# Four consecutive tokens to a partition in the router of a fused retention and mixture-of-experts kernel

## The chip, the cores and the metric

The kernel runs on one core of one Trainium2 chip. The metric is the device time of one execution in microseconds (us), the median of several runs.

The engines are named as the profile names them: PE is TensorE (matmul), PEld its weight loads, DVE is VectorE, ACT is ScalarE, POOL is GpSimd, SP is SyncE, which here only issues DMA transfers. A line number such as L471 points into the kernel that was profiled; the same statement has another number in another version.

## The reference, cut to what matters

```python
# attention: q, k, v are (8 batches, 8 heads, 576 tokens, 64)
scores = matmul(q, k.T) / sqrt(64)
ret = scores * Dmat[head]            # causal, decays as gamma[head] ** distance
x = matmul(ret, v)                   # -> (4608 tokens, 512)

# mixture of experts: 8 experts, 512 -> 1024 -> 512
logits = x @ w_gate
noisy  = logits + log1p(exp(x @ w_noise)) * noise     # noise: (4608, 8)
top2   = the two largest of noisy, with softmax weights
out[t] = sum over its two experts e of  weight * (relu(x[t] @ w1[e]) @ w2[e])
```

## The kernel before: the parts that matter

Attention is done in 16 **units** (a batch and half of its heads), four for each pair of batches. After a pair is done, its 1152 tokens are **routed**: gate logits, noise, top two, the place of each token in its expert's list. A route is a generator, and its pieces are put between the pieces of the next four units. A route holds its tokens as 9 columns of 128. After the third and the fourth route five **early** tiles of experts run between the pieces of the fourth route, then the 35 remaining tiles, the **expert stage**.

One unit's step in program order, cut:

```python
for n in range(NU + 1):
    if u + 4 < NU:
        at.load(u + 4, (nc.sync,) * 3)         # raw_q, raw_k, raw_v: 1.57 MB a unit
    if n in (1, 2):
        rt.load_noise(n - 1)                   # two batches of 9 transfers
    at.scores(u, 0)                            # PE; DVE masks the scores out of PSUM
    step()                                     # a piece of the pending route
    at.out(p)                                  # previous unit: x = S v, ACT copies it to xT
    at.tr(u + 1, "q")                          # PE transposes, ACT copies QT
    at.scores(u, 1)
    at.cast(u + 2)                             # POOL: kn, qb; ACT: vn from raw_v
    at.tr(u + 1, "k")                          # ACT copies KT
    at.states(u)
    ...
```

In the traces each engine takes its instructions in the program's order. A late raw_v thus holds ACT in `cast`, and the KT behind it, which the next unit's scores need (PE waits 2.97 us for KT at 49.1 us).

The four parts that the change touches (cuts marked with "..."):

```python
# (1) noise: 16 transfers of 32 partitions x 8 batches x 32 bytes, and two for the tails
nq = nm[:, :512, :].rearrange("b (c q r) e -> q r b c e", q=32, r=4)
for r in (2 * j, 2 * j + 1):
    for c in range(4):
        nc.sync.dma_start(out=self.noise[r * 32:r * 32 + 32, :, c, :], in_=nq[:, r, :, c, :])
nc.sync.dma_start(out=self.noiset[j * HD:(j + 1) * HD], in_=nt[:, j])

# (2) a route's rows of x: PE transposes back, ACT takes them out of PSUM (9 a route)
nc.scalar.activation(xr[c // 3][:, c % 3, :DM // 2].bitcast(BF16), pt, Act.Copy)

# (3) one-hots, twice a route; PE multiplies oh by olo to invert the permutation
V.tensor_tensor(olo[:, j], self.iota..., lo[:, j]..., Alu.is_equal)
for c in range(C):                             # C = 9
    V.tensor_scalar(oh[:, j, c, :], self.iota[:, :NH], hi[:, j, c:c + 1], K["local"][:, c:c + 1],
                    Alu.is_equal, Alu.mult)

# (4) ahead of the expert stage: gathers of its first tiles into attention's raw_q buffers
for i in range(3):
    xg = raw.tile([P, 2, 4, P], F32, name="raw_q")...
    nc.gpsimd.memset(xg, 0.0)
    for s in range(2):
        gather(tc, keep, xd, xg, i, s)
    pre.append(xg)
```

The raw_q buffers are four; the five early tiles use them too. The expert stage has a buffer "xg" of its own for the tiles that are not pre-gathered.

## Time and profile before

| | before |
|---|---|
| time, median of the first 3 runs | 514.96 us (514.65 to 515.98) |
| span of the profiled run | 515.2 us |
| mean granted PE clock | 0.900 |
| 0 to 49 us, start and units 0 to 3 | 49.1 us |
| 49 to 177 us, units 4 to 15 with three routes | 127.7 us |
| 177 to 231 us, fourth route and early experts | 54.1 us |
| 231 to 242 us, the first tile of the expert stage | 11.1 us |
| 242 to 515 us, the rest of the expert stage | 273.1 us |

The prediction below shows the lines on which its argument rests. Here are four others: from the page of the kernel before the totals, two of its slice rows (each digit is the busy share, or the granted clock, of one fortieth of the span in tenths), and the group of the rows of x (line, engine, operation, out<-in, shapes, count; then busy us, ns of one; then idle time ahead of it).

```profile
PE 420.6 (82%) x4587; PEld 304.6 (59%) x4627; DVE 248.4 (48%) x685; ACT 282.6 (55%) x429; POOL 278.9 (54%) x389
...
PE   0576777687589487895999999999999999999960
...
PEclk9999578666767699898999999999999999999995
...
L492 ACT ACTIVATE xr<-tr 128x512 bf16<-128x512 bf16 x36 | 21.3, 594 | 3.8 <-issue 2.9
```

The total of 82% hides two stages. PE is full from the 20th slice on, and hardly anywhere to the left of it; there its clock (the share of full speed that the throttle granted) is only 0.5 to 0.7 in many slices. Only the left half can give time to a change outside the expert stage.

### The profile page before, as it was taken

The numbers are of one execution on the slowest core, as the hardware profiler recorded it, in microseconds if no ns is written. First come the engines' busy times: TensorE is split into PE (matmuls) and PEld (weight loads), VectorE is DVE, ScalarE is ACT, GpSimd is POOL, SyncE is SP. The second block draws the span as 40 slices with busy tenths as digits, with TensorE's granted clock in tenths as the row PEclk, the third lists the DMA queues.
The fourth block names the chain that finished last, engine by engine and source line by source line (L and its number), as shares of the span: only waits on it lengthen the run. The fifth ranks groups of instructions, "written<-read, shape, count | busy, mean of one in ns | idle before, by whom it ended". The sixth has DMA issues, their size and how long they took to land.

```text
span 515.2 us, 11707 instructions
## 1 busy us (share of the span) xinstructions
PE 420.6 (82%) x4587; PEld 304.6 (59%) x4627; DVE 248.4 (48%) x685; ACT 282.6 (55%) x429; POOL 278.9 (54%) x389
## 2 busy tenths in 40 slices
PE   0576777687589487895999999999999999999960
PEld 0465566465467365654676666766767667666630
DVE  4333288658847838611233434534434445444440
ACT  3477598487669267352567656664655653332200
POOL 3674257517734616485045653745747777777440
PEclk9999578666767699898999999999999999999995
DMA  8996889996881904245568787797888855546320
GB/s 243 260 248 157 212 212 311 297 247 160 188 142 22 234 23 161 94 119 165 180 213 268 251 304 268 247 307 249 282 293 279 306 202 180 181 147 187 128 122 3
DMA packets 96169, 104.19 MB, mean 202 GB/s; under 512 B 25447, under 2 KB 73064, under 8 KB 96112
## 3 DMA queue, kind: packets, MB, share of 16 engines
q1 hardware_dynamic: 79824, 69.51, 45.2%
q0 software_dynamic: 14176, 32.83, 22.9%
q10 hardware_dynamic: 2112, 1.08, 0.8%
q8 instruction: 37, 0.61, 0.5%
q14 instruction: 20, 0.16, 0.1%
HBM read 84.66 MB, written 28.72 MB: 220 GB/s over the span
## 4 chain that ended last, share of the span: by engine, by line
PE 52%; DVE 6%; POOL 3%; issue 3%; DMA 1%; ACT 1%; POOLq 0%; DVEq 0%
PE p L961 24%; PE po L981 22%; PE pt L945 3%; DVE oh L655 2%; POOL xg L838 1%; DVE olo L651 1%; PE T L395 1%; PE x L405 1%; POOL raw_q L838 1%; DMA raw_q<-xd,xi 1%; DMA out_dram<-o,ix 1%; DVE S L266 0%; POOL xg L865 0%; PE R L666 0%; ACT raw_v L387 0%
## 5 line engine op out<-in xcount | busy, mean ns | idle before, releaser
L961 PE MATMUL p<-xgT,w 128*128 128x256 bf16 x1120 | 212.3, 274 | 3.6 <-DVE hT L968 1.9
L981 PE MATMUL po<-w,hT 128*128 128x512 bf16 x525 | 197.8, 381 | 0.1
L961 PEld LDWEIGHTS <-w 128*128 128x128 bf16 x1120 | 109.9, 98 | 72.9 <-issue 3.0
L968 DVE TENSOR_SCALAR hT<-p 128x512 bf16<-128x512 f32 x70 | 48.3, 691 | 141.8 <-PE p L961 141.8
L966 ACT ACTIVATE hT<-p 128x512 bf16<-128x512 f32 x70 | 41.8, 597 | 126.3 <-PE p L961 101.2
L1028 POOL DMA_INDIRECT out_dram<-o,ix x45 | 45.6, 1014 | 57.2 <-DVE o L1022 49.3
L838 POOL DMA_INDIRECT xg<-xd,xi x64 | 65.5, 1023 | 19.2 <-issue 11.7
L990 POOL DMA_INDIRECT prv<-yd,ix x45 | 45.2, 1004 | 37.6 <-DMA yd<-y 24.3
L266 DVE TENSOR_TENSOR S<-S,mask 128x1024 bf16<-128x1024 f32 x32 | 39.1, 1221 | 50.2 <-PE S L261 50.2
L981 PEld LDWEIGHTS <-hT 128*128 128x128 bf16 x560 | 55.0, 98 | 7.7
L911 ACT ACTIVATE w<-wst 128x1024 bf16<-128x1024 f32 x48 | 47.9, 1047 | 0.0
L196 POOL TENSOR_TENSOR kn<-raw_k,kg 128x1024 bf16<-128x1024 f32 x14 | 26.6, 1902 | 34.3 <-DMA raw_k<-in_k_dram 20.6
L948 ACT ACTIVATE xgT<-pt 128x1024 bf16<-128x1024 bf16 x35 | 35.6, 1018 | 1.4 <-PE pt L945 1.4
L1022 DVE SCALAR_TENSOR_TENSOR o<-po,g,prv 128x512 f32<-128x512 f32 x45 | 31.6, 742 | 0.8 <-PE po L981 0.8
L559 POOL TENSOR_TENSOR cum<-cum,M 128x16 bf16<-128x16 bf16 x36 | 8.2, 228 | 36.9 <-DVE d L562 34.4
L261 PE MATMUL S<-QT,KT 64*64 64x128 bf16 x512 | 17.1, 268 | 12.3 <-ACT KT L248 7.2
L201 ACT ACTIVATE vn<-raw_v 128x1024 bf16<-128x1024 f32 x16 | 16.9, 1056 | 18.1 <-DMA raw_v<-in_v_dram 11.9
L204 POOL TENSOR_TENSOR qb<-raw_q,qg 128x1024 bf16<-128x1024 f32 x14 | 26.6, 1900 | 0.0
L246 PE MATMUL tr<-ident,qb 128*128 128x128 bf16 x128 | 14.3, 278 | 14.5 <-DVE qb L204 13.1
L285 PE MATMUL T<-vn,kn 64*64 64x64 bf16 (+2 forms) x512 | 25.3, 243 | 0.0
L491 PE MATMUL tr<-ident,xT 128*128 128x128 bf16 x144 | 17.8, 262 | 8.6 <-ACT xr L492 8.1
L492 ACT ACTIVATE xr<-tr 128x512 bf16<-128x512 bf16 x36 | 21.3, 594 | 3.8 <-issue 2.9
(214 smaller groups left out, 633.4 us busy)
## 6 DMA issues: line engine op xcount, KB each, us to landing
wst<-in_moe_w_dram SPq DMA_DIRECT2D x48, 512.0 KB, 6.1
raw_k<-in_k_dram SPq DMA_DIRECT2D x32, 256.0 KB, 6.2
raw_v<-in_v_dram SPq DMA_DIRECT2D x32, 256.0 KB, 6.7
yd<-y SPq DMA_DIRECT2D x16, 512.0 KB, 3.6
raw_q<-in_q_dram SPq DMA_DIRECT2D x14, 512.0 KB, 5.5
xd<-xr SPq DMA_DIRECT2D x12, 396.0 KB, 5.3
w<-in_moe_w_dram POOLq DMA_DIRECT2D x4, 1024.0 KB, 8.2
yd<-raw_v SPq DMA_DIRECT2D x5, 512.0 KB, 3.5
```

What stands on the lines that cost most here:

```text
L196: eng.tensor_tensor(kn.rearrange("p r c h d -> p (c h) r d"), d.pop("rawk").rearrange("p c h (r d) -> p (c h) r d", r=2), self.kg[:, hq].r ...
L266: nc.vector.tensor_tensor(S.rearrange("p h c r t -> p (h c) (r t)"), p.rearrange("p h (c r) t -> p (h c) (r t)", r=2), self.K["mask"].rear ...
L838: tc.nc.gpsimd.indirect_dma_start(out=xg[:, s, :], out_offset=None, in_=xd[:, :], in_offset=IOff(ap=keep["xi"][:, j:j + 1], axis=0), bound ...
L911: nc.scalar.activation(W[e][:, k * F:(k + 1) * F], t, Act.Copy)
L948: return lambda: nc.scalar.activation(xgT, pt, Act.Copy)
L961: nc.tensor.matmul(p1[:, f2, :], lhsT=w[:, o:o + P], rhs=xgT[:, di, :], start=(di == 0), stop=(di == KD - 1))
L966: nc.scalar.activation(hT[:, 2 * fp:2 * fp + 2, :], p1, Act.Relu)
L968: V.tensor_relu(hT[:, 2 * fp:2 * fp + 2, :], p1)
L981: nc.tensor.matmul(po[s], lhsT=hT[:, fi, s * P:(s + 1) * P], rhs=w[:, o:o + DM], start=(fi == 0), stop=(fi == KF - 1))
L990: nc.gpsimd.indirect_dma_start(out=prv[i % NP][:, s, :], out_offset=None, in_=yd[:rows, :], in_offset=IOff(ap=st[i]["ix"][:, s, 1:2], axis=0),
L1022: V.scalar_tensor_tensor(o[:, s, :], st[i]["po"][s], st[i]["g"][:, s:s + 1], prv[i % NP][:, s, :], Alu.mult, Alu.add)
L1028: ins = nc.gpsimd.indirect_dma_start(out=out[:, :], out_offset=IOff(ap=st[i]["ix"][:, s, 0:1], axis=0), in_=st[i]["o"][:, s, :], in_offset ...
```

## The change

Its intent: a column of the router is to hold one of four places of 128 groups of four consecutive tokens. Then the four tokens' noise lies in 128 contiguous bytes and comes with one transfer instead of sixteen. For that, ACT's copy of x out of PSUM, which puts tokens in their order, is split in two. Beside it, four other things: the nine small DVE operations of a one-hot become two large ones; the rows of x leave PSUM by DVE instead of ACT; one tile instead of three is pre-gathered into raw_q buffers; the zeroing of a part of yd moves from the start to unit 12, and every unit takes one more piece of the route (two of the nine rows also change places among the pieces, which the cut leaves out). The diff, cut:

```diff
-    K["local"] = cp.tile([P, NC9], F32, name="local")
+    K["local"] = cp.tile([P, NC9], F16, name="local")
 ...
-            nc.scalar.activation(xv, p[e], Act.Copy)
+            xi = p[e].rearrange("p y c (r q) -> p y c r q", r=4)
+            for y in range(2):
+                nc.scalar.activation(xv[:, y], xi[:, y], Act.Copy)
 ...
-        for r in (2 * j, 2 * j + 1):
-            for c in range(4):
-                nc.sync.dma_start(out=self.noise[r * 32:r * 32 + 32, :, c, :], in_=nq[:, r, :, c, :])
-        nc.sync.dma_start(out=self.noiset[j * HD:(j + 1) * HD], in_=nt[:, j])
+        q.dma_start(out=self.noise.rearrange("p b r e -> p b (r e)"),
+                    in_=nm[:, :512, :].rearrange("b (p r) e -> p b (r e)", r=4))
+        for j in range(2):
+            q.dma_start(out=self.noiset[j * HD:(j + 1) * HD], in_=nt[:, j])
 ...
-            nc.scalar.activation(xr[c // 3][:, c % 3, :DM // 2].bitcast(BF16), pt, Act.Copy)
+            V.tensor_copy(xr[c // 3][:, c % 3, :DM // 2].bitcast(BF16), pt)
 ...
-            for c in range(C):
-                V.tensor_scalar(oh[:, j, c, :], self.iota[:, :NH], hi[:, j, c:c + 1], K["local"][:, c:c + 1],
-                                Alu.is_equal, Alu.mult)
+            V.tensor_tensor(oh[:, j], self.iota[:, :NH].unsqueeze(1).to_broadcast(sh),
+                            hi[:, j].unsqueeze(2).to_broadcast(sh), Alu.is_equal)
+            V.tensor_tensor(oh[:, j], oh[:, j], K["local"].unsqueeze(2).to_broadcast(sh), Alu.mult)
 ...
-        nc.sync.dma_start(out=yd[:P, :], in_=at.Tb[3]...)
 ...
-            if n in (1, 2):
-                rt.load_noise(n - 1)
+            if n == 1:
+                rt.load_noise(nc.sync)
 ...
-            if n >= NU - 2:
-                piece()
+            piece()
+            if n == NU - 4:
+                nc.sync.dma_start(out=yd[:P, :], in_=zero)
 ...
-        for i in range(3):
+        for i in range(1):
             xg = raw.tile([P, 2, 4, P], F32, name="raw_q")...
```

More of the change, by code (lines that the diff above doesn't have):

```diff
@@ L89, in constants @@
     K["tok"] = cp.tile([P, 4, NC9], F32, name="tok")
-    for r in range(4):
-        for b in range(2):
-            nc.gpsimd.iota(K["tok"][r * 32:r * 32 + 32, :, 4 * b:4 * b + 4], pattern=[[1152, 4], [P, 4]],
-                           base=r + 576 * b, channel_multiplier=4, allow_small_or_imprecise_dtypes=True)
+    for b in range(2):
+        nc.gpsimd.iota(K["tok"][:, :, 4 * b:4 * b + 4], pattern=[[1152, 4], [1, 4]], base=576 * b, channel_multiplier=4,
+                       allow_small_or_imprecise_dtypes=True)
     for h in range(2):
@@ L322, in out @@
             xv = self.xT[bp][:, 2 * hq:2 * hq + 2, 4 * b:4 * b + 4, :].rearrange(
-                "p y (c e) t -> p y c e t", e=2)[:, :, :, e, :]
-            nc.scalar.activation(xv, p[e], Act.Copy)
+                "p y r (c e q) -> p e y c r q", c=2, e=2)[:, e]
+            xi = p[e].rearrange("p y c (r q) -> p y c r q", r=4)
+            for y in range(2):
+                nc.scalar.activation(xv[:, y], xi[:, y], Act.Copy)
     def scores_tail(self, bp, hq):
@@ L465, in __init__, with load_noise @@
                     nc.vector.memset(t[:, 0, e:e + 1], float(k * TS))
-    def load_noise(self, j):
-        nc = self.nc
+    def load_noise(self, q):
         nm = self.moe_noise.rearrange("(b s) e -> b s e", b=8)
-        nq = nm[:, :512, :].rearrange("b (c q r) e -> q r b c e", q=32, r=4)
+        q.dma_start(out=self.noise.rearrange("p b r e -> p b (r e)"),
+                    in_=nm[:, :512, :].rearrange("b (p r) e -> p b (r e)", r=4))
         nt = nm[:, 512:, :].rearrange("(p b) s e -> s b p e", b=2)
-        for r in (2 * j, 2 * j + 1):
-            for c in range(4):
-                nc.sync.dma_start(out=self.noise[r * 32:r * 32 + 32, :, c, :], in_=nq[:, r, :, c, :])
-        nc.sync.dma_start(out=self.noiset[j * HD:(j + 1) * HD], in_=nt[:, j])
+        for j in range(2):
+            q.dma_start(out=self.noiset[j * HD:(j + 1) * HD], in_=nt[:, j])
     def route(self, bp):
@@ L512, in route @@
         yield
+        row(2)
         yield
@@ L535, in route @@
         V.tensor_add(nl, nl, lg[:, :, :E])
-        row(2)
         yield
@@ L594, in route @@
         G.tensor_copy(pl[:, :, 3], K["tok"][:, bp])
+        row(6)
         yield
-        row(6)
         pr = self.bank[:, :C * 2 * E].rearrange("p (c a e) -> p c a e", c=C, a=2)
@@ L653, in route @@
             yield
-            for c in range(C):
-                V.tensor_scalar(oh[:, j, c, :], self.iota[:, :NH], hi[:, j, c:c + 1], K["local"][:, c:c + 1],
-                                Alu.is_equal, Alu.mult)
-                if c == 4:
-                    yield
+            sh = [P, C, NH]
+            V.tensor_tensor(oh[:, j], self.iota[:, :NH].unsqueeze(1).to_broadcast(sh),
+                            hi[:, j].unsqueeze(2).to_broadcast(sh), Alu.is_equal)
+            yield
+            V.tensor_tensor(oh[:, j], oh[:, j], K["local"].unsqueeze(2).to_broadcast(sh), Alu.mult)
+            yield
             yield
@@ L1140 @@
         rt = Router(tc, actx, K, at, wgn, moe_noise, xd, keep)
-        nc.sync.dma_start(out=yd[:P, :], in_=at.Tb[3].rearrange("p a b c -> p (a b c)").bitcast(F32))
         NU = 16
@@ L1160, in step @@
                 more()
+        zero = at.cp.tile([P, DM], F32, name="zero")
+        nc.gpsimd.memset(zero, 0.0)
         at.cast(0, nc.vector)
```

## The prediction

> **What bounds the kernel now.** I read the page's slices first, then busy time by stretch, then the timelines of the stretches where TensorE (PE) is not full. The stretch view (length; busy us of PE, weight load, DVE, ACT, POOL; granted clock; DMA share; GB/s) divides the 515 us:
>
> ```profile
> 49.00:61.00 12.00, 8.57 (x183) 6.51 (x184) 4.12 (x5) 7.50 (x12) 4.04 (x3) 0.57 0.67 155
> 85.00:97.00 12.00, 6.18 (x160) 4.97 (x158) 11.86 (x35) 8.41 (x12) 8.78 (x12) 0.92 1.13 318
> 109.00:121.00 12.00, 10.20 (x174) 7.97 (x175) 9.13 (x27) 11.16 (x17) 4.67 (x11) 0.64 1.14 311
> ...
> 177.00:231.00 54.00, 46.07 (x400) 32.70 (x404) 27.20 (x111) 31.20 (x50) 25.52 (x49) 0.94 0.33 104
> 231.00:242.00 11.00, 5.48 (x56) 4.53 (x57) 1.88 (x11) 3.13 (x4) 7.22 (x11) 1.00 0.40 104
> 242.00:505.00 263.00, 253.66 (x1869) 175.95 (x1902) 110.05 (x288) 130.21 (x173) 149.85 (x150) 0.99 0.68 229
> ```
>
> The last 263 us, the experts, have PE busy 96% at clock 0.99, and the change touches nothing there. All that can be won lies before 242 us, where no single engine is full throughout. Three places in it carry the argument.
>
> First, 40 to 62 us. The DMA issues of the SP queue (start, duration, what, count) are back to back, and the two batches of noise loads stand in front of the attention loads of the next units:
>
> ```profile
> 40.75 6.62 SPq L475 DMA_DIRECT2D noise<-in_moe_noise_dram  x8
> 47.41 1.16 SPq L476 DMA_DIRECT2D noiset<-in_moe_noise_dram  x1
> 48.67 0.55 SPq L173 DMA_DIRECT2D raw_q<-in_q_dram  x1
> ...
> 51.76 5.87 SPq L475 DMA_DIRECT2D noise<-in_moe_noise_dram  x8
> 57.66 0.70 SPq L476 DMA_DIRECT2D noiset<-in_moe_noise_dram  x1
> 58.47 0.56 SPq L173 DMA_DIRECT2D raw_q<-in_q_dram  x1
> ```
>
> The loads pay for it: the view of waits shows POOL and ACT waiting for them, and PE's timeline then waits for ACT, because ACT runs in order and its cast of a late raw_v stands in front of the copy of KT that the scores need.
>
> ```profile
> POOL kn L196 <- DMA raw_k<-in_k_dram: 20.6, 5, 6.5
> ACT vn L201 <- DMA raw_v<-in_v_dram: 11.9, 3, 5.4
> ...
> 49.14 0.42 PE L261 MATMUL S<-QT,KT 64*64 64x128 bf16 x16 [2.97 <-ACT KT L248]
> 59.40 0.64 PE L261 MATMUL S<-QT,KT 64*64 64x128 bf16 x16 [2.35 <-ACT KT L248]
> ```
>
> Of a unit of attention one sees 5.8 us between first scores at full clock (29.1 to 35.2 to 40.9 us), and 8.2 and 10.3 us in this place (40.9 to 49.1 to 59.4).
>
> Second, where a route builds its one-hots, DVE is full (11.86 of 12 us at 85 to 97). For the third route this holds up PE, and the fourth route repeats it at 204 to 208 (3.6 us idle):
>
> ```profile
> 174.34 2.49 DVE L655 TENSOR_SCALAR oh<-R,hi,local 128x80 f16<-128x80 f32 x9
> 176.88 0.76 PE L666 MATMUL R<-oh,olo 128*128 128x80 f16 x9 [4.71 <-DVE oh L655]
> ```
>
> Third, the start of the experts. The third pre-gathered tile waits for a raw_q buffer that an early tile still holds, so its gather starts 23 us after the first one's (212.8) and PE waits for it:
>
> ```profile
> 235.70 1.01 POOL L838 DMA_INDIRECT raw_q<-xd,xi  x1 [0.27 <-POOL raw_q L1228]
> 239.84 0.40 PE L945 MATMUL pt<-ident,raw_q 128*128 128x128 bf16 x4 [0.71 <-DMA raw_q<-xd,xi]
> 242.09 0.59 PE L961 MATMUL p<-xgT,w 128*128 128x256 bf16 x2 [1.85 <-DVE hT L968]
> ```
>
> **What the Trainium skill says.** "DMA: Bandwidth & Descriptors", Specifications, puts line rate at 512 B or more per descriptor. The noise comes in 32-byte pieces before and 128-byte pieces after: still short, but a quarter as many. The trace agrees in kind: 8 KB here takes the queue about 0.8 us (6.62 / 8), a 512 KB raw_q 0.55 us when the queue is free. "VectorE: DVE Perf Modes", The perf-mode tier table, gives a tensor_copy out of PSUM at most twice the basic rate and tensor_tensor with PSUM the basic rate. The second agrees: olo, 1152 elements with an fp32 PSUM source, steps at 1.27 us, 1.1 ns an element. The first no instruction here shows; ACT's 594 ns for the row is the comparison. "TensorE: Matmul & The Clock Gate", Part 1, halves PE's clock after an idle window of about 3.4 us. The trace agrees: granted 1.00 to 50 us, then 0.50 for 53 to 63 us, after the two waits. "SBUF — State Buffer", Who interferes with whom, lets a DVE op with two SBUF inputs block against a GpSimd op reading SBUF. The trace agrees: two 9-element DVE ops take 1.50 and 1.83 us at 76.8 and 78.3 us, ending with POOL's kn and qb.
>
> **The change part by part.**
> 1. Noise and yd. Eighteen issues (6.62 + 1.16 + 5.87 + 0.70 = 14.4 us of SP) become three. The large one has 128 x 8 = 1024 pieces against raw_q's 512 at 0.55 us, so about 1.1 us, plus the two tails as before, 1.9: 3 us. The zeroing of yd (1.75 us at 24.3) moves to an SP that waits idle after 129 us. The unit loads that now start at 48.7 and 58.5 start at about 42 and 45 to 46, or, since the DMA is then full at 300 GB/s and a unit has 1.57 MB (5.2 us), land near 50 and 55. First scores at 49.1, 59.4, 70.2 and 82.2 become about 47, 54, 62 and 71. The last interval I leave long, as the route's own stalls there stay. After that compute, not loads, paces the units, so the lead should last: **-11 us**, and it may also keep PE warm.
> 2. Rows of x. 36 copies of 594 ns leave ACT (-21.3 us in all, 5.3 a route). On DVE they are 0.35 to 0.6 us each: 3.2 to 5.4 us a route. The one-hots shrink: nine tensor_scalars step 2.42 us, the comparison of 720 elements at 1.1 ns is 0.8 and the product as much, so 1.6: 0.8 saved twice a route. DVE is thus up by 1.6 to 3.8 us a route.
> 3. Copies of x out of PSUM. The four-token order splits each in two: 383 ns for 256 elements (the tails' copy of that shape) twice against 595 once, +0.17 us x 32 = +5.5 us of ACT. ACT is still down by 16 us. In units 9 to 12 it was 93% busy (11.16 of 12), so it helps there; DVE, in order and carrying the score masks, now also waits for the transposes. Net over three routes: **-2 us**.
> 4. Third route. A piece more per unit lets it begin its one-hots a little sooner; they are 1.6 us shorter, but three rows (1 to 1.8 us) now lie on the same DVE chain. Of PE's 4.7 us wait: **-2 us**.
> 5. Fourth route, 177 to 231 us. PE has 46 us of work in 54 and cannot go lower. ACT no longer mixes rows with relus; one-hots are 1.6 us shorter: **-2.5 us**.
> 6. Pre-gathers 3 to 1: the second and third tile gather into buffers of the expert stage, whose gathers already start at 215 us. PE's g1 ends at 236.9 and the next group starts at 242.1. Of these 5.2 us, 0.7 remain for a transpose: **-4.5 us**.
>
> Sum -22, which would be 493 us. Since the parts follow each other and a lead can be eaten by a later wait, I take a seventh off: **496 us**.
>
> **Rivals.** (a) DVE becomes the bound. A route's DVE work is about 17 us plus four units' masks at 2.44 us and tails, some 28.5 us per four units; it becomes 30 to 32, or 7.5 to 8 us a unit, against 9.8 us a unit now. That speaks against a full DVE, but it is full already in the one-hot stretch. If the masks wait there, items 2 and 4 turn to +5 us: about 503. (b) The loads' lead is swallowed: DMA is already saturated at 84 to 103 and 107 to 121 us. For it: share above 1.1 there. Against: these loads run up to four units ahead; the last lands near 125 us and is cast at 153. If half is lost: 501. (c) PE stays warm from 50 us on and units run at 7 us while loads allow: 487. (d) The product of one-hots, with two SBUF inputs, blocks behind POOL's casts for up to 1.9 us, twice a route: +3 us at most.
>
> **Range and chances.** Items 1 and 6 make -15 with clear mechanisms; the rest ranges from +6 to -13. Some 8 in 10: 486 to 506 us. The 2% line is 504.7 us; only (a) and (b) together reach it. Faster 0.86, same 0.12, slower 0.02.
>
> **What would show it.** Item 1: SP issues three noise loads in about 3 us, and first scores of units 5 to 7 come 5, 8 and 11 us earlier; if the later units close that gap, (b) holds. Item 2: copies of xr on DVE at 0.35 to 0.6 us. Item 4: PE's wait for oh before R below 3 us. Item 6: no pre-gather after 230 us and no 5 us hole before the second expert group. The prediction is wrong if DVE's busy share over 60 to 170 us nears 95% and units take over 10 us, or if the expert stage itself changes length by more than 2 us.

## The result, and the profile after

A ratio in this document is the mean time of one kernel's runs over the mean of the other's in the same rounds, so it is not quite the ratio of the medians quoted beside it. Executions over 1.5% slower than the fastest of the same kernel are left out of the means. A gain in us is worked out as (1 - ratio) times the median of the kernel before in the same rounds.

| | before | after |
|---|---|---|
| median (range), 4 runs each | 515.47 (514.65 to 517.7) | 500.15 (499.07 to 503.46) |
| ratio, 95% interval | | 0.9707 (0.965 to 0.9764) |
| profiled span, mean clock | 515.2, 0.900 | 497.5, 0.907 |

The change is faster by 15 us; the profiled run by 17.7 us. The page of the kernel after, the same rows as before:

```profile
PE 411.8 (83%) x4587; PEld 298.9 (60%) x4627; DVE 255.6 (51%) x665; ACT 266.6 (54%) x425; POOL 281.6 (57%) x382
...
PE   0566968868575687989999999999999999999950
...
PEclk9969586686699599999999999999999999999995
```

DVE took on 7.2 us, ACT gave up 16.0 us, and PE's busy time fell by 8.8 us although it runs the same 4587 matmuls. So no work was saved there; single matmuls took less time, and the mean granted clock is the higher one. PE is full from about the 19th slice on now.

Where the time came from is read off PE's timelines of both kernels, at eight places that are the same work in both, and at the end:

| start of | before | after | difference | length of the stage before and after |
|---|---|---|---|---|
| unit 4's scores | 49.1 | 48.7 | -0.4 | 49.1, 48.7 |
| unit 7's scores | 82.2 | 76.4 | -5.8 | 33.1, 27.7 |
| unit 12's scores | 131.1 | 122.2 | -8.9 | 48.9, 45.8 |
| unit 15's scores | 165.0 | 154.2 | -10.8 | 33.9, 32.0 |
| third route's product with oh | 176.9 | 163.5 | -13.3 | 11.9, 9.4 |
| first early tile's transposes | 177.4 | 167.9 | -9.5 | 0.6, 4.4 |
| expert stage, first transposes | 231.0 | 219.6 | -11.4 | 53.6, 51.7 |
| expert stage, second group | 242.1 | 226.0 | -16.1 | 11.1, 6.4 |
| end | 515.2 | 497.5 | -17.7 | 273.1, 271.5 |

So the lead grows to 13.3 us, loses 3.8 us, and then gains 1.9 us in the fourth route, 4.7 us at the start of the expert stage and 1.6 us behind that. These are single profiles. In three others, the changed kernel's second one and those of two kernels that differ from it only later (three pre-gathered tiles, earlier gathers; see the experiments), unit 5 starts at 59.0 to 59.3 us and unit 7 at 77.1 to 78.1. So the lead at unit 7 is 4 to 6 us, and the profile shown is at its upper end. The stretches of the kernel after (start:end, length; busy us of PE, PEld, DVE, ACT, POOL with counts; granted clock; DMA share, the mean busy share of the 16 DMA engines, which can come out above 1 in this view; GB/s):

```profile
49.00:61.00 12.00, 11.04 (x228) 8.83 (x217) 5.80 (x9) 8.46 (x18) 7.53 (x4) 0.57 1.13 308
...
81.00:93.00 12.00, 8.86 (x182) 7.45 (x180) 10.34 (x11) 7.77 (x12) 8.91 (x7) 0.78 1.04 305
...
109.00:121.00 12.00, 10.62 (x178) 8.07 (x176) 11.72 (x27) 7.78 (x14) 9.99 (x15) 0.60 0.43 122
163.50:219.50 56.00, 45.94 (x399) 32.21 (x404) 29.66 (x110) 27.42 (x42) 29.57 (x57) 0.91 0.46 148
...
226.00:488.00 262.00, 252.05 (x1869) 175.32 (x1902) 110.03 (x287) 130.26 (x173) 152.59 (x151) 0.99 0.67 223
```

In 49 to 61 us PE's busy time went from 8.57 to 11.04 us and the DMA share from 0.67 to 1.13: the hole in the loads is gone, and the transfers run at 308 GB/s. The second row reaches past the first route's one-hots, and its 10.34 us of DVE (11.86 before) don't mean that DVE is less full there: the one-hots and the mask between them take DVE from 79.4 to 88.2 us, 8.8 us, where they took it from 87.6 to 96.2, 8.6 us, before, and over 76 to 88 us DVE is busy for 11.76 of 12 us.

The third row shows what the average of 51% hides. DVE is busy for 11.72 of 12 us in the units of the second route, in a window where the kernel before has 9.13 (the prediction's third row), and in the whole from 95.6 to 129.8 us it never pauses for half a microsecond; the longest such stretch of the kernel before, up to 180 us, is 19.8 us. Part of this is time in which DVE stands blocked behind POOL (below). From unit 7 to unit 12, the same work in both, DVE is busy for 39.6 of 45.8 us, before for 35.8 of 48.9. So in the units with a route DVE is the fullest engine now. The last two rows hold nearly the same PE work as before (46.07 and 253.66 us there).

The SP queue of the kernel after, at the place that the prediction showed (start, duration):

```profile
41.39 1.13 SPq L471 DMA_DIRECT2D noise<-in_moe_noise_dram  x1
42.57 2.86 SPq L475 DMA_DIRECT2D noiset<-in_moe_noise_dram  x2
45.52 0.55 SPq L172 DMA_DIRECT2D raw_q<-in_q_dram  x1
...
49.58 0.46 SPq L172 DMA_DIRECT2D raw_q<-in_q_dram  x1
```

The noise takes 4.0 us of SP instead of 14.4. The next two units' loads are issued from 45.5 and 49.6 us on instead of 48.7 and 58.5. The waits for them shrink, in the view of waits (engine, what, for what: us in total, times, longest):

```profile
POOL kn L195 <- DMA raw_k<-in_k_dram: 13.8, 5, 4.3
...
ACT vn L200 <- DMA raw_v<-in_v_dram: 7.8, 3, 5.6
...
PE tr L490 <- DVE xr L491: 5.5, 6, 1.6
```

The first was 20.6 us and the second 11.9. The third is new in name: PE's row transposes wait for DVE's copies of rows, where before they waited 8.1 us in all for ACT's. The copy itself, from the page's groups:

```profile
L491 DVE COPY xr<-tr 128x512 bf16<-128x512 bf16 x36 | 15.1, 420 | 18.3 <-PE tr L490 7.8
```

It takes 420 ns where ACT took 594. PE's timeline at the later places (idle time ahead of an entry stands in brackets with what ended it):

```profile
57.84 0.64 PE L260 MATMUL S<-QT,KT 64*64 64x128 bf16 x16
...
128.75 0.66 PE L666 MATMUL R<-oh,olo 128*128 128x80 f16 x9 [3.00 <-DVE oh L657]
...
163.54 0.76 PE L666 MATMUL R<-oh,olo 128*128 128x80 f16 x9 [0.68 <-DVE oh L654]
167.91 1.01 PE L388 MATMUL tr<-ident,raw_q 128*128 128x128 bf16 x8 [3.61 <-DMA raw_q<-xd,xi]
```

Unit 5's scores start at 57.8 us without the wait for KT. The third route's wait for oh went from 4.71 to 0.68 us. Two waits are new. The early tile's gather isn't there yet when PE comes for it, 3.61 us. And the second of the second route's two products waits 3.00 us (in the kernel before the first of them waited 1.84) for DVE's multiplication, whose entry on DVE's timeline is this:

```profile
124.22 4.47 DVE L657 TENSOR_TENSOR oh<-oh,local 128x720 f16<-128x720 f16 x1
```

In the third route the same instruction takes 0.91 us, in the first two 1.56 to 1.77 otherwise. POOL's timeline at the same time:

```profile
124.17 1.89 POOL L195 TENSOR_TENSOR kn<-raw_k,kg 128x1024 bf16<-128x1024 f32 x1
126.03 1.89 POOL L203 TENSOR_TENSOR qb<-raw_q,qg 128x1024 bf16<-128x1024 f32 x1
```

POOL began 0.05 us before DVE did and ended with qb at 127.9; DVE's multiplication ended 0.8 us later, so it lay behind both.

Finally, PE at the start of the expert stage:

```profile
225.30 0.61 PE L945 MATMUL pt<-ident,xg 128*128 128x128 bf16 x8
225.96 0.38 PE L961 MATMUL p<-xgT,w 128*128 128x256 bf16 x2
```

The second tile comes out of xg and isn't waited for. The group that started at 242.1 us with 0.59 us for an entry, after a hole behind which PE's clock was granted at 0.50 (242 to 245 us; 1.00 before), now starts right behind the transposes with 0.38 us for an entry, at full clock.

### The profile page after: what moved, and what is told of

Read it like the earlier page. It is cut to its first block, busy times and chain, and to the rows that moved or that the text cites.

```text
span 497.5 us, 11662 instructions
## 1 busy us (share of the span) xinstructions
PE 411.8 (83%) x4587; PEld 298.9 (60%) x4627; DVE 255.6 (51%) x665; ACT 266.6 (54%) x425; POOL 281.6 (57%) x382
## 4 chain that ended last, share of the span: by engine, by line
PE 57%; DVE 3%; issue 1%; POOL 1%; ACT 1%; DMA 1%; POOLq 0%; ACTq 0%
PE p L961 26%; PE po L981 23%; PE pt L945 3%; PE x L407 2%; PE S L397 1%; PE T L397 1%; DMA out_dram<-o,ix 1%; DVE olo L650 1%; POOL cum L558 0%; DVE xr L491 0%; DVE oh L654 0%; PE tr L388 0%; ACT xgT L948 0%; ACT raw_v L389 0%; POOL out_dram L1028 0%
## 5 line engine op out<-in xcount | busy, mean ns | idle before, releaser
L968 DVE TENSOR_SCALAR hT<-p 128x512 bf16<-128x512 f32 x70 | 48.4, 692 | 142.0 <-PE p L961 142.0
L838 POOL DMA_INDIRECT xg<-xd,xi x68 | 69.6, 1024 | 20.2 <-issue 13.0
L1028 POOL DMA_INDIRECT out_dram<-o,ix x45 | 45.7, 1016 | 57.1 <-DVE o L1022 49.2
L326 ACT ACTIVATE xT<-x 128x256 bf16<-128x256 f32 x64 | 19.4, 389 | 18.4 <-PE x L318 18.4
L203 POOL TENSOR_TENSOR qb<-raw_q,qg 128x1024 bf16<-128x1024 f32 x14 | 28.7, 2052 | 0.0
L290 ACT ACTIVATE Tb<-T 64x512 bf16<-64x512 f32 x32 | 18.9, 589 | 11.1 <-PE T L284 10.9
L491 DVE COPY xr<-tr 128x512 bf16<-128x512 bf16 x36 | 15.1, 420 | 18.3 <-PE tr L490 7.8
L490 PE MATMUL tr<-ident,xT 128*128 128x128 bf16 x144 | 15.8, 240 | 10.3 <-DVE xr L491 5.5
```

Source lines behind the costliest of these rows:

```text
L203: eng.tensor_tensor(qb.rearrange("p r h d -> p h r d"), d.pop("rawq").rearrange("p c h w -> p (c h w)").rearrange("p (h r d) -> p h r d", ...
L838: tc.nc.gpsimd.indirect_dma_start(out=xg[:, s, :], out_offset=None, in_=xd[:, :], in_offset=IOff(ap=keep["xi"][:, j:j + 1], axis=0), bound ...
L968: V.tensor_relu(hT[:, 2 * fp:2 * fp + 2, :], p1)
L1028: ins = nc.gpsimd.indirect_dma_start(out=out[:, :], out_offset=IOff(ap=st[i]["ix"][:, s, 0:1], axis=0), in_=st[i]["o"][:, s, :], in_offset ...
```

## The experiments

Twelve kernels were run, in three lots; each lot has its own runs of the kernel before. All twelve gave correct results. The gain of the changed kernel itself was 15.1 us in the first comparison, and 13.3 us when it was run again in the third lot (0.9764 of 563.77), so a difference of 2 us between lots is not a finding. "Undoing costs" below is the range from 13.3 to 15.1 less the gain of the kernel named. It is no confidence interval: the gains have 95% intervals of 1.6 to 2.9 us to each side, so by the times alone a cost of under some 3 us isn't clear of nothing.

### Lot 1: one part of the change undone

**Noise in eighteen transfers again**, in the new order of tokens:

```diff
-        q.dma_start(out=self.noise...(r e), in_=...)              # one of 128 KB
+        for k in (2 * i, 2 * i + 1):
+            for r in range(4):
+                q.dma_start(out=self.noise[k * 32:k * 32 + 32, :, r, :], in_=nq[k * 32:k * 32 + 32, r])
-            if n == 1:
+            if n in (1, 2):
```

> The changed kernel, but its noise comes in eighteen transfers of 32-byte pieces in two batches again, as before the change (same order of tokens, same result). Theory: the lead of the attention units comes from the loads; the first scores of unit 7 came 5.8 us earlier in the changed kernel (76.4 against 82.2 us), so undoing this costs 4 to 6 us (504 to 506 us), and unit 7 starts near 82 us again. Rival: the lead comes from the relief of ACT in the route, and loads are hidden by later waits: within 1.5 us of the changed kernel (about 500 us).

Measured: 505.44 against 514.24 us, ratio 0.9811 (0.9768 to 0.9853), a gain of 9.7 us. Undoing costs 3.6 to 5.4 us. The SP queue of this kernel has the two batches back:

```profile
40.56 6.27 SPq L475 DMA_DIRECT2D noise<-in_moe_noise_dram  x8
...
51.54 6.05 SPq L475 DMA_DIRECT2D noise<-in_moe_noise_dram  x8
```

Unit 5's scores start at 61.1 us and unit 7's at 81.6, near the 82.2 of the kernel before, and the expert stage starts at 225.7 instead of 219.6. So the lead of the early units does come from these issues, and most of it lasts to the expert stage.

**Rows of x on ACT again.** One line:

```diff
-            V.tensor_copy(xr[c // 3][:, c % 3, :DM // 2].bitcast(BF16), pt)
+            nc.scalar.activation(xr[c // 3][:, c % 3, :DM // 2].bitcast(BF16), pt, Act.Copy)
```

> The changed kernel, but the rows of x leave PSUM on ACT again. Theory: the move was worth some 2 us (as predicted), so this takes about 502 us. Rival: DVE carries the score masks and is the fuller engine (108.6 us busy of 163 between 16 and 179 us, ACT 103.5), so the move hurt, and undoing it gives 497 to 499 us.

Measured: 502.48 against 514.24 us, 0.9764 (0.973 to 0.9798), a gain of 12.1 us. Undoing costs 1.2 to 3.0 us. In its view of waits the row transposes wait for ACT twice as long as they waited for DVE (5.5 us):

```profile
PE tr L490 <- ACT xr L491: 11.3, 7, 2.7
```

The expert stage starts at 223.2 us, 3.7 us later than in the changed kernel's first profile and 1.7 us later than in its second. That is the time that was expected (502 us), but it isn't clear of noise: the interval overlaps the changed kernel's, and the kernel with KT ahead of the cast (below), which has its rows on DVE, starts its expert stage at 222.5 us. What moving the rows to DVE is worth is not shown. It takes ACT out of the row transposes' way, but the copies now lie on the engine that is full in these units.

**Nine small operations for each one-hot again:**

```diff
-            V.tensor_tensor(oh[:, j], self.iota..., hi..., Alu.is_equal)
-            V.tensor_tensor(oh[:, j], oh[:, j], K["local"]..., Alu.mult)
+            for c in range(C):
+                V.tensor_scalar(oh[:, j, c, :], self.iota[:, :NH], hi[:, j, c:c + 1],
+                                K["local32"][:, c:c + 1], Alu.is_equal, Alu.mult)
```

> The changed kernel, but the one-hots are built column by column with two-operation instructions again (2.42 us per half). Theory: the product of the whole-tensor form waits for POOL in routes one and two (1.77, 1.56, 1.76 and 4.47 us against 0.91 undisturbed), so these routes gain nothing and the undo costs only what routes three and four save, 0 to 2 us (500 to 502 us). Rival: the shorter form pays 1.2 us per half where DVE is full, four routes, of which half is on the path: 4 us or more (504 us).

Measured: 501.74 against 514.24 us, 0.9753 (0.9717 to 0.9789), a gain of 12.7 us. Undoing costs 0.6 to 2.4 us by the times. The trace does not carry even that: this kernel's expert stage starts at 219.4 us, no later than in the changed kernel, and its longer span (499.0) comes from the first group of experts, 5.32 us at a lower clock instead of 3.66. The wait for oh in the third route is back to 2.49 us, but the gather behind it is then waited for only 1.27 us instead of 3.61, since it had more time. What two large one-hot operations are worth is not shown to differ from nothing.

**Three pre-gathered tiles again:**

```diff
-        for i in range(1):
+        for i in range(3):
```

> The changed kernel, but three tiles are gathered ahead into the loads' buffers again, as before. Theory: PE's hole of 5 us before the second expert group comes back, and with it a cold clock for 3 us after it: 5 to 6.5 us slower than the changed kernel, 505 to 506.5 us. Rival: the buffers would now be free early enough, or the hole is filled from elsewhere: under 2 us.

Measured: 506.85 against 514.24 us, 0.9832 (0.9795 to 0.9869), a gain of 8.6 us. Undoing costs 4.7 to 6.5 us, the largest of the four. PE's timeline has the hole back:

```profile
231.17 0.40 PE L945 MATMUL pt<-ident,raw_q 128*128 128x128 bf16 x4 [0.88 <-DMA raw_q<-xd,xi]
233.45 0.58 PE L961 MATMUL p<-xgT,w 128*128 128x256 bf16 x2 [1.67 <-DVE hT L968]
```

From the first transposes of the stage to the second group it takes 12.1 us, against 6.4 in the changed kernel (8.0 in its second profile) and 11.1 in the kernel before. In this profile and in that second one the clock was at 0.50 for a part of the first group too, so the hole itself makes some 4 us. The entry of 0.58 us shows the lower clock behind the hole as well (1.00 until 233 us, then 0.50 to 0.65 up to 236).

### Lot 2: one part alone, and what was lost

At this point the lead of the early units was half of what had been predicted. Two theories stood for it. **Theory C, the clock**: the units after 50 us run at half clock in the profile, which eats the lead. **Theory L, the loads**: the transfers themselves are at their limit, so loads issued earlier don't land as much earlier.

**The kernel before with the new order of tokens and the noise in three transfers alone** (its diff is the parts of tok, xT copies and load_noise of the change):

> The kernel before with the order of tokens alone changed: noise in three transfers, the copies of x out of PSUM each in two, rows on ACT, old one-hots, old pre-gather, old zeroing of yd. Theory: the loads' lead is worth 5 us less what 32 more copies on ACT cost (5.5 us busy, partly on the path): 511 to 513 us (ratio 0.992 to 0.996). Rival: without the relief of the rows ACT is so full in the route's units (93% at 109 to 121 us) that the copies eat the lead whole: 515 us or more.

Measured: 513.52 against 515.19 us, 0.9969 (0.9933 to 1.0005), a gain of 1.6 us, which is not clear of nothing. Unit 5's scores come at 57.1 us, as early as in the changed kernel (57.8), but unit 7's at 80.2 instead of 76.4, unit 12's at 128.3 instead of 122.2, and the third route's product at 175.2 instead of 163.5. So the parts don't add. The early lead is there and is eaten on the way, when ACT still carries the rows (row transposes wait 8.0 us in all for it), the one-hots are the old ones and a unit has a piece of the route less. Neither of the first two accounts for it alone: the kernel with rows on ACT has the product at 168.4 us and the one with the old one-hots at 163.8. That leaves the additional piece, the moved rows and the moved zeroing, or the parts together; no run tells these apart.

**KT ahead of the cast**, against theory C's cause, the wait that lets PE go cold:

```diff
-            if u + 2 < NU:
-                at.cast(u + 2)
             if u + 1 < NU:
                 at.tr(u + 1, "k")
+            if u + 2 < NU:
+                at.cast(u + 2)
```

> The changed kernel with two calls exchanged: in each unit ACT's copy of KT stands ahead of its cast of the v loaded for two units later, so a late load holds back no scores. Theory: half of the loads' lead was eaten because PE still waits 2.2 us at 48.7 us, its clock drops to half for 50 to 60 us, and units 4 and 5 then take 9.2 and 7.9 us at 93% PE busy. Without that wait PE should stay near full clock there and unit 7 should start 3 to 6 us earlier (70 to 73 us): 495 to 497 us in all. Rival: the lead is limited by the loads or by DVE, not by the clock: unit 7 within 1.5 us of 76.4, total within 1.5 us of the changed kernel's 500.

Measured: 501.78 against 515.19 us, 0.9754 (0.9717 to 0.9791), a gain of 12.7 us, so no better than the changed kernel. Unit 4's scores come 2.3 us earlier, at 46.3, without their wait for KT, but PE then waits in the next place for the same late ACT:

```profile
49.01 0.51 PE L318 MATMUL x<-QT,Tb 128*128 128x128 bf16 x6 [1.82 <-ACT Tb L290]
```

Unit 5's scores stay at 58.0 us and unit 7's at 76.7. The clock was low here again, so this run spoke against the order of ACT's work and didn't yet decide on the clock. The 495 to 497 us that were expected didn't come.

**The multiplication of the one-hot on POOL**, where it can't lie behind POOL's casts as another engine's operation:

```diff
-            V.tensor_tensor(oh[:, j], oh[:, j], K["local"]..., Alu.mult)
+            G.tensor_tensor(oh[:, j], oh[:, j], K["local"]..., Alu.mult)
```

> The changed kernel, but the product of the one-hots (two inputs in SBUF) runs on POOL instead of DVE. Theory: the product blocks DVE behind POOL's casts (up to 4.47 us) and PE then waits for the score masks behind it (1.67 and up to 2.31 us, once or twice a route), so moving it saves 2 to 4 us: 496 to 498 us. Rival: POOL in order delays its own casts and the gathers of the early tiles by the same time, and the route waits for POOL instead: within 1 us, or slower.

Measured: 502.49 against 515.19 us, 0.9767 (0.9737 to 0.9798), a gain of 12.0 us. The long stretch of 4.47 us is gone, POOL takes 1.39 us for each of them. Unit 12's scores start at 119.8 us and the third route's product at 160.4, 2.3 and 3.2 us earlier than in the changed kernel, although unit 7's came no earlier (76.9): with DVE's busy time over units 7 to 12 down from 39.6 to 34.4 us these five units take 42.9 us instead of 45.8 (44.3 in the changed kernel's second profile). So by these traces DVE sets the pace there. But the fourth route's product now waits for POOL,

```profile
199.95 0.48 PE L666 MATMUL R<-oh,olo 128*128 128x80 f16 x9 [1.82 <-POOL oh L657]
```

and the early gather, which is POOL's work too, is waited for 5.04 us instead of 3.61. The expert stage starts at 219.7 us, as before the edit. The stall was real, and taking it away on these terms doesn't pay: not the 496 to 498 us that were expected but the rival's outcome.

**The early gathers a unit earlier**, against the new wait of 3.61 us:

```diff
-            if n == NU - 2:
+            if n == NU - 3:
                 assert len(routed) >= 2
                 work.append(early(tc, K, at, keep, xd, yd, W, EARLY, routed))
-            if n in (NU - 2, NU - 1):
+            if n in (NU - 3, NU - 2, NU - 1):
                 more()
```

> The changed kernel, but the early tiles' gathers are asked for one unit earlier. Theory: PE's new wait of 3.6 us for the first early tile's gather (167.9 us; the gather left POOL at 158.2 and 159.7, behind the third route's work) goes: 496 to 497 us. Rival: PE is then held at the next place, the scores of the last units or the one-hots of route three, and gains under 1 us.

Measured: 499.88 against 515.19 us, 0.9714 (0.9681 to 0.9747), a gain of 14.7 us. The wait is gone:

```profile
158.89 0.63 PE L388 MATMUL tr<-ident,raw_q 128*128 128x128 bf16 x8
```

The expert stage starts at 217.7 us, 1.9 us earlier, and the profiled span is the shortest of all, 495.6 us. The times don't tell it from the changed kernel (496 to 497 us had been expected), so what the wait cost, some 2 us of the 3.6 by this one trace, is not shown by them.

### Lot 3: the clock against the loads

This lot ran on another chip, where both kernels were some 49 us slower (see below). All four of its kernels start their expert stage between 221.2 and 221.8 us, so the part that is asked about isn't touched by that. The changed kernel stood in this lot as its own control:

> The changed kernel unedited, to have it with more rounds and in the rounds of the next three: 500 us, ratio 0.967 to 0.974. Both theories say the same.

Measured: 550.68 against 563.77 us, 0.9764 (0.9721 to 0.9807), a little above the ratio that was expected. And it told much on the question: in this execution the clock over 48 to 60 us was 0.97, where the first profile of the same kernel had 0.60. PE was busy for 6.84 of these 12 us instead of 10.37, and unit 5's scores came later all the same, at 59.25 us instead of 57.84. ACT's timeline and then PE's show what they waited for:

```profile
55.36 1.06 ACT L200 ACTIVATE vn<-raw_v 128x1024 bf16<-128x1024 f32 x1 [2.27 <-DMA raw_v<-in_v_dram]
```

```profile
58.87 0.21 PE L497 MATMUL R<-wgn,xT 128*128 128x32 bf16 x2 [3.17 <-ACT xT L356]
```

Unit 6's raw_v lands at about 55.4 us, ACT casts it, does the KT, Tb and xT that stand behind it, and then PE may go on. With the clock low, PE's own work fills the same time. So the loads set the pace here and the clock doesn't, and DMA share over 48 to 60 us was 1.10 in this run and 1.12 in the first: the DMA engines have no idle time left in it.

The two executions ran on different chips, but the kept traces of the other runs say the same. Over all twelve profiles with the noise in three transfers the clock over 48 to 60 us lies between 0.56 and 1.00, and unit 5's scores start between 57.1 and 59.9 us without following it: 57.97 at a clock of 0.56 (KT ahead of the cast), 57.84 at 0.60 (the changed kernel's first profile), 59.02 at 0.97 (three tiles again, on the chip of lot 1), 57.92 at 1.00 (all three edits, below).

**40 more small matmuls in unit 3**, so that PE is kept warm on purpose:

```diff
+            if n == 3:
+                for _ in range(40):
+                    nc.tensor.matmul(rt.bank[:, :P], lhsT=K["ident"], rhs=K["ident"], start=True, stop=True)
```

> The changed kernel with 40 useless matmuls (identity by identity, into a part of a PSUM bank that nobody has in use yet) where PE waits at 46.3 to 48.7 us, so that PE isn't idle there. Theory: PE's clock drops to half at 50 us because of that wait, and at half clock PE is 93% busy and eats the loads' lead; with the wait filled the clock stays at 0.9 or more over 50 to 60 us and unit 7 starts 2 to 5 us before 76.4: 496 to 498 us. Rival one: the clock stays up but units 5 to 7 are held by the loads (DMA share 1.13 there) or by DVE: clock 0.9 or more, unit 7 within 1 us, total as the changed kernel. Rival two: the clock drops all the same (the sparse 48.7 to 50 us is enough): nothing is told.

Measured: 549.8 against 563.77 us, 0.974 (0.9707 to 0.9774), a gain of 14.7 us against the control's 13.3, within both intervals. The clock over 48 to 60 us was 0.98, unit 5's scores came at 59.1 and unit 7's at 77.9 (control 59.25 and 78.1). As the control was as warm without the matmuls, this run alone tests little; with the clocks and starts just listed theory C falls.

**Noise issued from POOL's queue**, which takes the remaining 4 us from SP:

```diff
-                rt.load_noise(nc.sync)
+                rt.load_noise(nc.gpsimd)
```

> The changed kernel with its three noise loads issued from POOL's queue in place of SP's. Theory: SP spends 4.0 us on them (1.13 and 2.86) right ahead of unit 6's loads, which unit 5 needs; these then start at about 41.5 in place of 45.5 us. If loads bind, unit 5 starts 2 to 3 us earlier and the total falls by 1 to 3 us; if PE at half clock binds (rival), unit 5 stays within 0.7 us of 57.8 and the total within 1 us.

Measured: 550.12 against 563.77 us, 0.9751 (0.9708 to 0.9794), a gain of 14.0 us. Unit 5's scores came at 59.0 and unit 7's at 76.95, 1.1 us before the control's. The 2 to 3 us at unit 5 that the loads were expected to give didn't come; the 0.3 us that came are the number of the rival, but the clock by which the rival explained it had no bearing in the list above. The traces show why issuing earlier gained so little. SP issued unit 6's loads from 41.6 us on instead of 45.8, but ACT's cast of unit 6's raw_v began only 0.9 us earlier (54.5 against 55.4), and the one of unit 5's, whose loads now share the DMA engines with them, 1.4 us later (48.4 against 47.0). With the DMA engines full an earlier issue moves the wait from one unit to another, which is what theory L says.

**All three, warm PE, noise on POOL and the earlier gathers:**

```diff
+                for _ in range(40): nc.tensor.matmul(...)
-                rt.load_noise(nc.sync)
+                rt.load_noise(nc.gpsimd)
-            if n in (NU - 2, NU - 1):
+            if n in (NU - 3, NU - 2, NU - 1):
```

> The changed kernel with three edits at once: useless matmuls in PE's wait before unit 4, noise on POOL's queue, early tiles' gathers asked for one unit earlier. Theory: the gains of the three add where they lie in different stages: 3 to 6 us under the changed kernel, 494 to 497 us. Rival: DVE and PE in the route's units are full enough to swallow the early ones, and only the gathers' 2 us remain: 498 us.

Measured: 551.48 (with the slow run, 556.65; the ratio is without it) against 563.77 us, 0.9759 (0.972 to 0.9798), a gain of 13.6 us, the control's, and nothing of the 3 to 6 us that were expected. Unit 7's scores came at 76.0 us, 2.1 us earlier than the control's, but unit 12's at 122.55 against 122.43. Eight profiles show the same (the changed kernel's two, old one-hots, three tiles, earlier gathers, and the three other kernels of this lot): unit 7 starts between 76.0 and 78.1 us, unit 12 between 122.2 and 122.7. DVE is full in between, so the early differences are taken up there. Of all kernels only the one with the multiplication on POOL has unit 12 earlier (119.8). No version that was run beats the changed kernel by a difference clear of noise.

**What stays open.** Why lot 3 was slower: the expert stage took 328 us instead of 278 in the changed kernel's profile, with waits of DVE and ACT marked "remote" (78.5 and 59.6 us in all) and waits of PE's weight loads marked "issue" (34.6 us) that the first chip's profile doesn't have. The busy time of its DVE and ACT operations is the same, and the kernel before was slower by as much. It is seen on one chip, and none of the runs looks into it. Also open are the shares of the moved zeroing of yd, of the additional piece and of the split copies, which were not run alone.

## Why the prediction was right or wrong, point by point

The prediction said 496 us, in 486 to 506, and faster with a chance of 0.86. The time is 500.15 us, in the range, and the kernel is faster. By its own items, in the profiled runs: the sum was -22 and the span fell by 17.7 us. That the total comes so close is partly luck, since items that gave 9.1 us less than said and items that gave 4.8 us more offset each other. Neither of its signs of being wrong appeared: DVE's share over 60 to 170 us was 83% (90.95 of 110 us), units took 9.8 us from unit 6 to unit 15, and from its second group on the expert stage changed by 1.6 us.

**1. Noise and yd, -11 predicted: half of it came.** This is the term that was mis-sized. The trace has -1.6, -4.4 and -5.8 us at units 5, 6 and 7 (-0.2, -3.1 and -4.1 with the second profile), where the prediction had about -5, -8 and -11, and putting the transfers back costs 3.6 to 5.4 us. The step that failed is "unit loads that now start at 48.7 and 58.5 start at about 42 and 45 to 46, or ... land near 50 and 55". They started at 45.5 and 49.6. The large noise issue took 1.13 us, as its estimate from the count of pieces said (about 1.1). Of the 3.5 us at the first, 2.4 are that moving the zeroing of yd freed no SP time at this place (the noise starts at 41.39 instead of the 39.0 that the prediction's sum has; it was 40.75), and 1 us is that the two tails took 2.86 us instead of 1.9. And they landed later than "near 50": unit 6's raw_v at about 53.7 us in the first profile of the changed kernel and 55.4 in the second. From the first issue to this landing it took 8.2 and 9.6 us, where the prediction's 5.2 are 1.57 MB at 300 GB/s with nothing else under way; but unit 7's loads were issued from 49.6 us on, before unit 6's had landed. The prediction knew the limit and yet reckoned each unit's loads alone. Its rival (b), "If half is lost: 501", is what happened, though not by later units: the loads of the very next ones are at the limit (308 GB/s, share 1.13). The remark that the lead "may also keep PE warm" was of no consequence: the clock was 0.60 in one execution and 0.97 in another, with unit 5 no earlier in the second. Nor does the trace agree with the idle window of about 3.4 us as the prediction read it: the clock fell at about 50.8 us, between the two waits and not after both, behind an idle time of 2.97 us, and in the second profile of the changed kernel it fell at 42.3 us behind a wait of 0.6 us. And its "agrees in kind" on the 512 B compares how long SP is held, not a rate of transfer. The 5.8 us of a unit at full clock are 6.1 and 5.8.

**2. Rows on DVE: right in kind.** The copies took 420 ns (0.33 to 0.36 us until the next operation starts), the lower end of the 0.35 to 0.6 that was said. At 512 elements that is 0.64 to 0.70 ns an element, against 1.1 for the comparison olo that the prediction measured: nearer twice the rate than once, as "VectorE: DVE Perf Modes", The perf-mode tier table, allows at most for a copy out of PSUM. Rival (a) came true in part. Averaged over the stages DVE is no bound: 108.4 us busy of the 163 between 16 and 179 us, 66%. But in the units of the second route it is full, as shown above, and sets their pace. The prediction's 7.5 to 8 us a unit against 9.8 was such an average too, and left out the time in which DVE is blocked behind POOL. What didn't come is the loss of 5 us that (a) gave to items 2 and 4: the lead still grew. Undoing costs 1.2 to 3.0 us by the times, not clear of noise.

**2 and 3, net -2 by the prediction:** from unit 7 to unit 15 the lead grew by 5.0 us. The split copies of x were nearly free: four take 1.21 us of ACT together where two took 1.09, as their times in the trace overlap, and so 16 units cost some 2 us of ACT and not 5.5. The kernel with the noise and the order alone shows another side: without the other parts the early lead doesn't last (1.6 us in the end), so the items are no independent terms, as the prediction's sum took them to be. Which of the parts keeps it is open, and that the growth of 5.0 us is due to items 2 and 3 is read from one profile (4.8 us with the second) and not shown by undoing them.

**4. Third route, -2:** the wait for oh fell from 4.71 to 0.68 us as the prediction asked (below 3), and PE's lead at this place rose by 2.5 us. But the time was given back at once: a wait of 3.61 us for the first early gather. This wait the prediction didn't have. A gather that had been hidden by the wait taken away came into view, the loss of 3.8 us in the table. Gathering a unit earlier removes it.

**5. Fourth route, -2.5:** 1.9 us came, from 53.6 to 51.7 us.

**6. Pre-gathers, -4.5:** more came. The hole closed, which is 4.7 us, and the group behind it runs at full clock, 1.6 us further. The test gave 4.7 to 6.5 us by the times, and some 4 us for the hole at equal clock. The prediction had seen the hole and the buffer that made it, but not that the hole also cost the clock of the group behind it.

**Rival (d), DVE's multiplication against POOL,** was real and larger in one place than said: 4.47 us instead of "up to 1.9", since two casts in a row went first. PE waited 3.00 us for it once. It is inside the +3 us given there.

The shortfall of 4.3 us in the profiled runs is thus 5.2 of item 1, 3.3 of item 4 and 0.6 of item 5, less 3.0 more in items 2 and 3 and 1.8 more in item 6.

## What to carry to other kernels

Here sixteen small transfers on the queue that also issues the large loads held up the loads behind them (14.4 us of SP with the tails, 4.0 after); gather them into one by choosing the layout. When a place has waited for its loads, work out how soon they can land at the bandwidth the trace shows, and let that bound the gain. Buffers taken from a pool that another stage still holds turn a prefetch into a wait: look at when each gather was issued, not at how many there are; and when a wait is taken away, look at what the same engine needs next. When work is moved to another engine, look at that engine in the stage where it is fullest, not at its average.

## What the Trainium skill lacked or had wrong

- "DMA: Bandwidth & Descriptors" gives the time of a transfer and of its completion. On how long an issue holds the issuing queue it has only a cycle count per copy for "previous generations", in a table on a later chip, and nothing on how the time grows with the number of pieces or with busy DMA engines. Here 16 transfers of 8 KB held SP for 12.5 us, one of the same bytes in all 1.13 us. A pair of raw_k issues took 1.05 us behind the noise in the kernel with eighteen transfers and 3.46 us where the DMA share was above 1 (the changed kernel's second profile).
- "SBUF — State Buffer", Who interferes with whom, says that the later of DVE and GpSimd blocks for the whole instruction. Here the block lasted over two GpSimd instructions in a row: an operation of 0.91 us took 4.47. The page has no such case.
- "TensorE: Matmul & The Clock Gate", Part 1, describes a free-running window, and so a start that differs from run to run. In the middle of a kernel there is a spread as well, whose cause no run looks into: over the same 12 us one kernel was granted 0.60 in one execution and 0.97 in another (on another chip), and the first group of the expert stage took 3.66 or 5.32 us in two kernels that do the same there. This is a spread of 1.7 us that is not the change's.
- No page has what made the expert stage 50 us longer in the third lot, with waits marked "remote" of 78.5 us on DVE.
